# Four of twelve opening filler products on TensorE split into forty 64x64 products

## The chip, the cores and the metric

The kernel runs on one core of one Trainium2 chip. The metric is the device time of one execution in microseconds, from the first to the last thing the core does for it. Three runs of the kernel before gave 791.76, 792.56 and 793.32 us; the median is 792.56 us. Engines are named as in the profile: PE is TensorE's matmul row, PEld its weight load, DVE is VectorE, ACT is ScalarE, POOL is GpSimd, SP is SyncE. An engine's name with a q behind it (SPq, POOLq) is its instruction queue issuing DMAs.

## The reference

Chunked softmax attention on `q`, `k`, `v` of shape 8 x 8 x 576 x 64 (batch, head, position, channel) is followed by a feed-forward layer over the 4608 x 512 result:

```python
q_c, k_c, v_c = (x.reshape(B, H, nc, 64, D) for x in (q, k, v))   # nc = 9 chunks of 64
scores = scale * np.matmul(q_c, k_c.transpose(0, 1, 2, 4, 3))
attn = softmax(scores)                       # over the 64 keys of the same chunk
x = np.matmul(attn, v_c)                     # then laid out as 4608 tokens x 512
h = x @ w_in                                 # 512 -> 2048
g = np.where(h >= 1, h, np.where(h <= -1, 0, (h + 1) ** 2 / 4))
return g @ w_out                             # 2048 -> 512
```

All arrays are float32. The kernel gets near float32 precision out of a faster matmul type by splitting each operand into a high and a low part and adding three products.

## The kernel before, in words

The tokens are worked on in nine tiles of 512. For the first tile (`t = 0`), four pairs of heads are loaded, turned by TensorE against an identity matrix (`flip`, L547, four 128x128 transposes into a PSUM bank), copied to SBUF by ScalarE (L560), multiplied into 64x64 score blocks (`attn_products`, L579), put through a softmax on VectorE, ScalarE and GpSimd (L658 to L674), turned back (L547, copied at L684), multiplied with `v` (L600) and split into a high and a low part (L737, L738). Meanwhile the weights arrive as raw words (`load_weight`, L418, L425) and are split by ScalarE and VectorE (`prepare`, L442 to L471). The feed-forward products of the first three tiles are L788 (in) and L823 (out); later tiles run in pairs through a scheme with fewer products (L1060).

The order on every engine is fixed when the program is built. `Plan.add` collects pieces of work with an engine, an assumed cost and what they need; `Plan.run` places them in time by a list schedule, and calls each piece's `emit` in that order. Each engine then executes its own stream strictly in that order, waiting on semaphores.

Where the plan thinks that TensorE would stand idle early in the program, it puts in a filler: `fill()` in `Plan.run` picks one from a list of (emit, begin, end), and the plan books 0.215 us for it at full pace. A filler is one product of the 128x128 identity (`ident`) with itself into a PSUM bank that real work will overwrite later (`warm`, L1473). Two kinds exist: into `ps_h0` from the start until the first real product of that bank, and into `ps_o0` after that. No result uses a filler's output, and it reads only `ident`, which GpSimd writes first (masks.py:197 and 199). In the profile each float32 product is two passes, and each pass is one weight load (PEld) and one matmul (PE); a transpose is one pass.

The first thing on TensorE is twelve fillers in a row. Behind them stand the transposes of the first pair's `k` and `q`, then fillers and real work in turn.

Of the kernel before, what the change touches and what calls it, by code (L numbers as in the profile page):

```python
# [261 lines left out]
def kernel(  # L262
# [15 lines left out]
    nc = tc.nc  # L278
# [5 lines left out]
    C = 64  # L284
# [12 lines left out]

    EARLY = 2

    BATCH = (0, 1, 2, 3, 4, 5, None, 6, 7)  # L300


# [15 lines left out]
    def buffers(pool, name, n, dtype=F32):  # L318
        return [
            (f"{name}{i}", pool.tile([P, T], dtype, name=f"{name}{i}")) for i in range(n)  # L320
        ]

    ident = sb.tile([P, P], F32, name="ident")
# [43 lines left out]
    h_banks = buffers(psum, "ps_h", 2)  # L367
# [31 lines left out]
    plan = Plan()  # L399
# [79 lines left out]
    def heads_rows(src, t, h):  # L479


        if BATCH[t] is not None:
            return src[BATCH[t], h, :T, :].rearrange("(c p) d -> c p d", p=C)
        return src[:, h, T:, :]
# [10 lines left out]
    def load_blocks(dst, src, t, g, queue):  # L495
# [3 lines left out]
        for j in range(2):  # L499
            for i in range(2):  # L500
                r = (2 * j + i) * Q
                rows = heads_rows(src, t, 2 * g + j)[:, :, i * Q:(i + 1) * Q]
                if BATCH[t] is not None:
                    queue.dma_start(
# [10 lines left out]
    def load_values(dst, src, t, g, queue):  # L515

        for h in range(2):
            rows = heads_rows(src, t, 2 * g + h)
            into = dst[:, h * HALF:(h + 1) * HALF].rearrange("p (n d) -> p n d", d=D)
            if BATCH[t] is not None:  # L520
                queue.dma_start(out=into, in_=rows.rearrange("(n r) p d -> (r p) n d", r=2))
# [5 lines left out]
    def load_heads(t, g, which="qkv"):  # L527
        for n, src, bufs in (("q", q, q_bufs), ("k", k, k_bufs), ("v", v, v_bufs)):
# [4 lines left out]
            parts = 4 if load == load_blocks else 2  # L533
            if BATCH[t] is None:
                parts *= 2
# [297 lines left out]
    def store(t, s):  # L833
# [15 lines left out]
        def send():  # L849
            row = BATCH[t] * S + s * P  # L850
            nc.sync.dma_start(out=out[row:row + P, :], in_=o())
# [620 lines left out]
    def warm(bank):  # L1472
        return lambda: nc.tensor.matmul(  # L1473
            out=bank[:, :P], lhsT=ident, rhs=ident, start=True, stop=True
        )


    plan.emit(("pe", 0.215, 512, (
        (warm(h_banks[0][1]), None, plan.written["ps_h0"][0]),
        (warm(o_banks[0][1]), turned[0], plan.written["ps_o0"][NP]),  # L1480
    )))

# [30 lines left out]
```

## Time and profile before

| what | value |
|---|---|
| median of three runs | 792.56 us (791.76 to 793.32) |
| the profiled execution | 793.6 us, its span from first to last instruction 791.8 us |
| TensorE matmuls (PE) | busy 782.8 us, 99% of the span, 5626 instructions |
| TensorE weight loads (PEld) | busy 646.2 us, 82%, 5626 instructions |
| VectorE | 659.9 us, 83% |
| ScalarE | 523.4 us, 66% |
| GpSimd | 178.4 us, 23% |
| mean granted TensorE clock | 0.999 |

The times in the trace are counted from the span's start. The profiled execution took 1.8 us more than its span, and 1.0 us more than the median run. A matmul's end is modelled, so the starts of the weight loads are the safer clock for TensorE's pace. Where the trace merges instructions into one row, the row gives the first start and the time until the last end. "issue" as a releaser means that the profile shows nothing that the engine waited for.

### The profile page before, as it was taken

The numbers are of one execution on the slowest core, as the hardware profiler recorded it, in microseconds if no ns is written. First come the engines' busy times: TensorE is split into PE (matmuls) and PEld (weight loads), VectorE is DVE, ScalarE is ACT, GpSimd is POOL, SyncE is SP. The second block draws the span as 40 slices with busy tenths as digits, with TensorE's granted clock in tenths as the row PEclk, the third lists the DMA queues.
The fourth block names the chain that finished last, engine by engine and source line by source line (L and its number), as shares of the span: only waits on it lengthen the run. The fifth ranks groups of instructions, "written<-read, shape, count | busy, mean of one in ns | idle before, by whom it ended". The sixth has DMA issues, their size and how long they took to land.

```text
span 791.8 us, 15101 instructions
## 1 busy us (share of the span) xinstructions
PE 782.8 (99%) x5626; PEld 646.2 (82%) x5626; DVE 659.9 (83%) x1013; ACT 523.4 (66%) x903; POOL 178.4 (23%) x294
## 2 busy tenths in 40 slices
PE   9999999999999999999999999999999999999997
PEld 8788888878878888887887888888888888888886
DVE  4889998898679889998769999887699976755796
ACT  5998975444445456886579667865797658657851
POOL 1000005743234433222111112121112111211211
PEclk9999999999999999999999999999999999999999
DMA  9896869858799867898899879989766896666664
GB/s 207 221 359 152 252 136 289 290 174 234 190 277 278 219 170 232 246 299 229 225 243 240 225 210 271 273 226 241 204 198 185 220 260 207 191 192 191 183 207 106
DMA packets 254664, 177.16 MB, mean 224 GB/s; under 512 B 211968, under 2 KB 220160, under 8 KB 254592
## 3 DMA queue, kind: packets, MB, share of 16 engines
q0 software_dynamic: 33344, 117.98, 47.4%
q1 hardware_dynamic: 216992, 57.18, 32.0%
q10 hardware_dynamic: 4256, 1.05, 0.7%
q8 instruction: 44, 0.72, 0.4%
q14 instruction: 28, 0.23, 0.1%
HBM read 133.17 MB, written 38.80 MB: 217 GB/s over the span
## 4 chain that ended last, share of the span: by engine, by line
PE 83%; DVE 7%; ACT 4%; DMA 3%; SPq 1%; issue 1%; ACTq 0%; DVEq 0%
PE ps_o L1060 39%; PE ps_o L823 14%; PE ps_h L788 14%; PE ps_h L1060 12%; PE ps_a L579 2%; DMA aT_both<-qT_both 2%; PE ps_h L600 1%; DVE big_wo L1111 1%; DMA k_sb_both<-in_k_dram 1%; ACT big_wo L1110 1%; ACT big_wo L1107 1%; DMA words_wi<-in_moe_w_in_dram 1%; SPq L490 1%; SPq L722 0%; PE ps_o L600 0%
## 5 line engine op out<-in xcount | busy, mean ns | idle before, releaser
L968 POOL DMA_DIRECT2D big_wi<-mixed x144 | 76.8, 534 | 325.7 <-PE ps_o L1060 178.2
L788 PE MATMUL ps_h<-xh,parts_wi 128*128 128x512 f32 x376 | 123.9, 392 | 0.1
L823 PE MATMUL ps_o<-parts_wo,gh 128*128 128x512 f32 x384 | 119.5, 392 | 0.0
L1060 PE MATMUL ps_o<-big_wo,big_wi 128*128 128x512 f32 x396 | 95.6, 389 | 0.0
L1060 PE MATMUL ps_o<-gh,big_wi 128*128 128x512 f32 x264 | 88.6, 391 | 0.4 <-ACT big_wo L1075 0.3
L1060 PEld LDWEIGHTS ps_o<-big_wo,big_wi 128*128 128x128 f32 x396 | 74.3, 188 | 15.5
L788 PEld LDWEIGHTS ps_h<-xh,parts_wi 128*128 128x128 f32 x376 | 70.6, 188 | 16.5 <-DVE r L799 1.2
L823 PEld LDWEIGHTS ps_o<-parts_wo,gh 128*128 128x128 f32 x384 | 71.4, 188 | 15.3 <-issue 0.3
L1060 PE MATMUL ps_h<-big_wi,big_wi 128*128 128x512 f32 x312 | 75.9, 390 | 0.0
L823 PE MATMUL ps_o<-parts_wo,gl 128*128 128x512 f32 x192 | 74.8, 390 | 0.0
L788 PE MATMUL ps_h<-xl,parts_wi 128*128 128x512 f32 x188 | 73.3, 390 | 0.1
L1060 PE MATMUL ps_o<-big_wi,big_wi 128*128 128x512 f32 x282 | 70.8, 391 | 0.7 <-ACT tmp L1075 0.4
L1060 PEld LDWEIGHTS ps_h<-big_wi,big_wi 128*128 128x128 f32 x312 | 58.4, 188 | 12.2
L1167 ACT CAST big_wo<-big_wo 128x512 fp32r<-128x512 f32 x76 | 47.2, 622 | 31.6 <-PE ps_o L1060 19.9
L1060 PEld LDWEIGHTS ps_o<-big_wi,big_wi 128*128 128x128 f32 x282 | 52.6, 188 | 12.8 <-ACT tmp L1075 1.3
L1167 ACT CAST gh<-big_wo 128x512 fp32r<-128x512 f32 x76 | 47.2, 621 | 23.2 <-PE ps_o L1060 18.2
L1168 DVE TENSOR_TENSOR big_wo<-big_wo,big_wo 128x512 fp32r<-128x512 f32 x76 | 51.6, 684 | 11.6 <-ACT big_wo L1167 11.6
L1110 ACT ACTIVATE big_wo<-big_wo 128x512 f32<-128x512 f32 x96 | 59.8, 632 | 1.9
L1060 PEld LDWEIGHTS ps_o<-gh,big_wi 128*128 128x128 f32 x264 | 49.5, 188 | 12.0 <-ACT big_xl L753 0.8
L1168 DVE TENSOR_TENSOR gl<-big_wo,gh 128x512 fp32r<-128x512 f32 x76 | 51.6, 683 | 8.6 <-ACT gh L1167 8.5
L795 ACT ACTIVATE r<-ps_h 128x512 f32<-128x512 f32 x47 | 28.1, 597 | 36.4 <-PE ps_h L788 36.2
L1060 PE MATMUL ps_o<-gl,big_wi 128*128 128x512 f32 x132 | 51.4, 390 | 0.0
(269 smaller groups left out, 1648.9 us busy)
## 6 DMA issues: line engine op xcount, KB each, us to landing
big_wi<-mixed POOLq DMA_DIRECT2D x144, 512.0 KB, 4.7
big_wo<-mixed POOLq DMA_DIRECT2D x24, 512.0 KB, 4.3
words_wi<-in_moe_w_in_dram SPq DMA_DIRECT2D x16, 512.0 KB, 7.0
words_wo<-in_moe_w_out_dram SPq DMA_DIRECT2D x16, 512.0 KB, 8.8
v_sb<-in_v_dram SPq DMA_DIRECT2D x60, 128.0 KB, 4.0
q_sb_both<-in_q_dram SPq DMA_DIRECT2D x112, 64.0 KB, 3.9
k_sb_both<-in_k_dram SPq DMA_DIRECT2D x112, 64.0 KB, 3.1
mixed<-parts_wi POOLq DMA_DIRECT2D x24, 256.0 KB, 4.2
```

The lines of the kernel that those rows point to most:

```text
L490: queue.dma_start(out=dst[j * C:(j + 1) * C], in_=heads_rows(src, t, 2 * g + j).rearrange("c p d -> p c d"),)
L579: nc.tensor.matmul(out=scores[i * C:(i + 1) * C, half, n * C:(n + 1) * C], lhsT=qT[rows, at], rhs=kT[rows, at], start=True, stop=True,)
L600: nc.tensor.matmul(out=values[half][h * C:(h + 1) * C, n * C:(n + 1) * C], lhsT=v_sb[rows, of:of + C], rhs=rhs, start=True, stop=True,)
L788: nc.tensor.matmul(out=ps, lhsT=weight["wi", j][:, half, kc * P:(kc + 1) * P], rhs=x(), start=(kc == 0 and i == 0), stop=(kc == KC - 1 and ...
L795: plan.add("act", 0.48, lambda: nc.scalar.activation(out=r, in_=ps, func=AF.Relu, bias=0.5, scale=0.5), (pkey,), (rkey,))
L823: nc.tensor.matmul(out=acc, lhsT=x[:, cols], rhs=weight["wo", j][:, half, :], start=(j == 0 and i == 0), stop=(j == NF - 1 and i == 2),)
L968: nc.gpsimd.dma_start(out=place_of(tag).bitcast(F32), in_=mixed[n][:, rows, :])
L1060: nc.tensor.matmul(out=bank, lhsT=parts[part], rhs=rhs, start=fresh and begin and k == 0, stop=end and k == 2, skip_group_check=not fresh,)
L1107: plan.add("act", 0.5, lambda: nc.scalar.activation(out=r(), in_=h(), func=AF.Relu, bias=0.5, scale=0.5), (hkey,), (rkey,))
L1110: plan.add("act", 0.52, lambda: nc.scalar.square(out=r(), in_=r()), (), (rkey,))
L1167: plan.add("act", 0.52, lambda: nc.scalar.copy(out=h(), in_=x()), (key,), (hkey,))
L1168: plan.add("dve", 0.6, lambda: nc.vector.tensor_tensor(out=l(), in0=x(), in1=h().bitcast(F32), op=ALU.subtract), (key, hkey), (lkey,))
```

## The change

The first four calls of the filler into `ps_h0` no longer emit one 128x128 product. Each emits ten products of 64x64 blocks of the identity instead, alternating between the upper half (rows 0 to 63, result in partitions 0 to 63) and the lower half (rows 64 to 127, result in partitions 64 to 127). From the fifth call on the filler is what it was. The plan still books the same cost for each call, so that the order of everything else is the same.

```diff
+    OPENING, SMALL = 4, 5
...
+    fills = itertools.count()
+
+    def opening():
+        bank = h_banks[0][1]
+        if next(fills) >= OPENING:
+            return warm(bank)()
+        for half in [0, 1] * SMALL:
+            rows = slice(half * C, (half + 1) * C)
+            nc.tensor.matmul(out=bank[rows, :C], lhsT=ident[rows, :C], rhs=ident[rows, rows], start=True, stop=True)
+
     plan.emit(("pe", 0.215, 512, (
-        (warm(h_banks[0][1]), None, plan.written["ps_h0"][0]),
+        (opening, None, plan.written["ps_h0"][0]),
         (warm(o_banks[0][1]), turned[0], plan.written["ps_o0"][NP]),
     )))
```

This is the start of TensorE's stream before, from the program's first instruction to the first scores (products are counted here, not passes; `ps_h` is the bank that fillers write, `ps_o` takes the transposes, `ps_a` the scores):

```order
L1508 UNCONDITIONAL_BRANCH
L1473 MATMUL ps_h_93<-ident 128x128 x12
L547 MATMUL ps_o_92<-ident,k_sb_both 128x128 x4
L547 MATMUL ps_o_91<-ident,q_sb_both 128x128 x4
L1473 MATMUL ps_h_93<-ident 128x128 x4
L579 MATMUL ps_a<-kT_both,qT_both 64x64 x16
```

And this is the same place of TensorE's stream in the changed program, whose line numbers are 1 to 14 higher:

```order
L1519 UNCONDITIONAL_BRANCH
L1487 MATMUL ps_h_93<-ident 64x64 x40
L1474 MATMUL ps_h_93<-ident 128x128 x8
L548 MATMUL ps_o_92<-ident,k_sb_both 128x128 x4
L548 MATMUL ps_o_91<-ident,q_sb_both 128x128 x4
L1474 MATMUL ps_h_93<-ident 128x128 x4
L580 MATMUL ps_a<-kT_both,qT_both 64x64 x16
```

Forty small products have come in ahead, and eight of the twelve large ones are left behind them. That is 80 passes for 8, or 144 instructions more, counting weight loads and matmuls. The rest of TensorE's stream and the streams of the other four engines are the same, row for row.

## Rows read from the trace of the kernel before

**Rows 1.** The page: span, busy time, share and instructions of each engine.
```profile
span 791.8 us, 15101 instructions
PE 782.8 (99%) x5626; PEld 646.2 (82%) x5626; DVE 659.9 (83%) x1013; ACT 523.4 (66%) x903; POOL 178.4 (23%) x294
```
**Rows 2.** The chain that ended last, 0 to 30 us: start us, us, what.
```profile
1.50 4.51 DMA k_sb_both<-in_k_dram
...
10.48 4.79 DMA words_wi<-in_moe_w_in_dram
...
15.29 0.68 ACT tmp L442
...
17.06 0.54 DVE tmp L450
...
25.02 0.69 DVE xl L738
25.71 0.04 issue
25.75 1.43 PE ps_h L788 x5
```
**Rows 3.** Waits of TensorE's weight loads over the whole run: us, times, longest.
```profile
PEld ps_o L600 <- DMA k_sb_both<-in_k_dram: 0.4, 1, 0.4
```
**Rows 4.** Weight loads in order of time, 1.3 to 4.9 us: start, us, what.
```profile
1.37 3.70 PEld L1473 LDWEIGHTS ps_h<-ident 128*128 128x128 f32 x17 [1.37 <-POOL ident masks.py:199]
```
**Rows 5.** The same view, 4.95 to 6.9 us (its first load began earlier).
```profile
4.74 1.12 PEld L1473 LDWEIGHTS ps_h<-ident 128*128 128x128 f32 x8
```
**Rows 6.** All engines in order of time, 5.9 to 9 us.
```profile
6.12 0.42 PEld L547 LDWEIGHTS ps_o<-ident,k_sb_both 128*128 128x128 f32 x4 [0.27 <-issue]
...
6.95 0.97 PEld L1473 LDWEIGHTS ps_h<-ident 128*128 128x128 f32 x8
...
8.04 0.56 PEld L579 LDWEIGHTS ps_a<-kT_both,qT_both 64*64 64x64 f32 x32
...
8.66 0.42 PEld L547 LDWEIGHTS ps_o<-ident,k_sb_both 128*128 128x128 f32 x4
...
8.80 0.69 DVE L658 TENSOR_REDUCE mx_both<-ps_a 128x8 f32<-128x512 f32 x1 [8.80 <-PE ps_a L579]
```
**Rows 7.** Weight loads in order of time, 7.9 to 8.6 us.
```profile
7.73 0.19 PEld L1473 LDWEIGHTS ps_h<-ident 128*128 128x128 f32 x1
```
**Rows 8.** Stretches: us, busy (count) of each engine, PEclk, DMA share, GB/s.
```profile
2.00:4.00 2.00, 2.00 (x11) 2.00 (x11) 0.00 (x0) 0.45 (x1) 0.00 (x0) 1.00 0.90 185
7.00:8.00 1.00, 1.00 (x10) 0.92 (x8) 0.00 (x0) 0.89 (x2) 0.00 (x0) 1.00 1.37 184
18.00:20.00 2.00, 2.00 (x46) 1.93 (x38) 1.93 (x5) 1.58 (x4) 1.04 (x1) 1.00 1.09 287
20.00:25.00 5.00, 4.73 (x87) 3.81 (x86) 4.93 (x9) 4.86 (x9) 1.04 (x1) 1.00 0.98 297
```
**Rows 9.** Groups by line and shape, 0 to 12 us: busy us, mean ns | idle us.
```profile
L579 PEld LDWEIGHTS ps_a<-kT_both,qT_both 64*64 64x64 f32 x32 | 0.6, 134 | 0.1
```
**Rows 10.** ScalarE in order of time, 6 to 26 us.
```profile
14.45 0.59 ACT L684 COPY aT_both<-ps_o 128x512 f32<-128x512 f32 x1
15.29 0.68 ACT L442 ACTIVATE tmp<-words_wi 128x512 f32<-128x512 f32 x1 [0.26 <-DMA words_wi<-in_moe_w_in_dram]
15.87 0.58 ACT L560 COPY first_wi<-ps_o 128x512 f32<-128x512 f32 x1
16.34 0.69 ACT L445 ACTIVATE words_wi<-words_wi 128x512 uint32<-128x512 uint32 x1
```
**Rows 11.** VectorE in order of time, 6 to 26 us.
```profile
17.06 0.69 DVE L450 SCALAR_TENSOR_TENSOR tmp<-tmp,words_wi 128x512 uint32<-128x512 uint32 x1 [0.89 <-ACT words_wi L445]
```
**Rows 12.** The page's DMA queues: packets, MB, share of 16 engines' span.
```profile
q8 instruction: 44, 0.72, 0.4%
```
**Rows 13.** Weight loads in order of time, 492 to 500 us.
```profile
497.73 0.45 PEld L579 LDWEIGHTS ps_a<-kT_both,qT_both 64*64 64x64 f32 x22
498.62 0.65 PEld L579 LDWEIGHTS ps_a<-kT_both,qT_both 64*64 64x64 f32 x34 [0.45 <-issue]
```
**Rows 14.** Weight loads in order of time, 184.8 to 185.9 us.
```profile
185.59 0.19 PEld L823 LDWEIGHTS ps_o<-parts_wo,gh 128*128 128x128 f32 x1 [0.27 <-issue]
```

## The prediction

> **What bounds the kernel now.** I read four views: the page's busy times, the chain that ended last, TensorE's weight loads in order of time through the first 9 us, and the streams of ScalarE and VectorE up to 26 us. TensorE is busy 99% of the span [rows 1], and from 25.75 us the chain is TensorE's own work with few breaks [rows 2]. So a delay of that point is a delay of the end, unless a later wait for a transfer takes it up. The only such wait on TensorE that the list names is 0.4 us long [rows 3]. Ahead of 25.75 us TensorE is not the bound: the chain goes through the landing of `k` at 6.01, a weight transfer landing at 15.27, then ScalarE's and VectorE's preparation of the weights [rows 2]. The question is what a slower or faster opening of TensorE does to that point.
>
> **The opening before.** Twelve fillers are 24 passes. Seventeen loads start from 1.37 on, the seventeenth at 4.74, where the next view begins [rows 4, 5]: (4.74 - 1.37) / 16 = 0.211 us a pass. Later eight passes of the same fillers take 0.97 us with 0.19 for the last load, so (0.97 - 0.19) / 7 = 0.111 us a pass [rows 6, 7]. The first pace is half the second: 1.2 against 2.4 GHz by the pace. The granted clock's column says 1.00 in both stretches [rows 8], so in the first microseconds I go by the pace. In the eight loads from 4.74 to a last start at 4.74 + 1.12 - 0.19 = 5.67, the seven steps sum to 0.93 us; 1.6 steps of 0.211 and the rest of 0.111 fit that, so the pace doubled at about 5.07, some 3.7 us after the first filler began [rows 5]. The last filler pass is through by 5.78, `k` has landed at 6.01, and the first transpose loads at 6.12 [rows 2, 6]. TensorE had some 0.3 us to spare here.
>
> **The change part by part.**
>
> *Removed:* 8 passes of 128x128 at the slow pace, 8 x 0.211 = 1.69 us.
>
> *Added:* 80 passes of 64x64. The trace has passes of that shape: 32 in the scores, whose loads take 0.56 us with 0.134 for one, so (0.56 - 0.13) / 31 = 0.0139 us a pass at the fast pace [rows 6, 9]. But the scores use four combinations of row half and output half, the new products only two (the upper with the upper, the lower with the lower). If what a pass holds is its quarter of the array, two quarters give half the rate: 0.0277 fast, 0.0555 slow. The ends: if the issue of instructions sets the 0.0139, two quarters cost no more than four (0.0278 slow); if the two halves do not overlap at all, a pass costs half of a large one, 0.0555 fast and 0.1055 slow. I take 0.0555 slow, 0.0277 fast.
>
> The Trainium skill, TensorEngine Tiling (Array Packing), "Key Properties", says that different tiles of the array execute loads and products in parallel, and the section on configurations counts four 64x64 tiles. By this rule a tile is the resource and two tiles run at half the rate of four, which is the value taken; the pace of the scores agrees with four in parallel, no row shows two.
>
> So from 1.37 to 5.07 there are 3.70 / 0.0555 = 67 passes, and the other 13 take 13 x 0.0277 = 0.36 us: 5.43. The change of shape costs a little: the last of the 32 score loads starts at 8.47, the next, larger one at 8.66 [rows 6], 0.15 more than the shape's own step, so 5.58. Sixteen passes of the eight remaining large fillers at 0.111 are 1.78 us: 7.36. The `k` transposes then load at 7.36 in place of 6.12: **+1.24 us**. The spare 0.3 us is used up in this. At the low end (0.0278 slow) the small ones end at 1.37 + 2.22 = 3.59, and 16 passes, the first 6 slow, end at about 6.1: no delay. At the high end 35 passes run by 5.07, 45 more take 2.50 us, then 0.15 and 1.78: 9.50, a delay of 3.4 us.
>
> *What a delay of 1.24 us does to 25.75 us.* The scores, the softmax and the turning back of the first heads follow TensorE, so ScalarE's copy at 14.45 moves to 15.69 and ends at 16.28. Then comes `prepare` at 15.29, which now waits for nothing but the copy. It had idled 0.26 us for the weight transfer [rows 10]: it is late by about 1.24 - 0.26 = 0.98. VectorE at 17.06 waits for the ScalarE step at 16.34, which is behind it in ScalarE's stream [rows 10, 11], so it is late by the same. From 18 to 25 us VectorE is busy 6.86 of 7.00 us, which leaves 0.14 us to catch up with [rows 8], and the chain runs on VectorE until 25.71 [rows 2]. I take **+0.97 us** at 25.75 and at the end. Should the slack at 15.29 not count (another copy, at 15.87, follows TensorE too), it is +1.24; with the 0.4 us of [rows 3] taken up as well, +0.57. The DMA issues on SP and ScalarE at the start load fresh buffers and wait for none of this.
>
> *Moved:* the program's blocks. 44 packets of 0.72 MB are 16 KB each [rows 12], and TensorE's 11,252 instructions [rows 1] by 44 are 256 each: 64 bytes an instruction. The 144 new ones shift every later block edge by 0.56 of a block against the work. Two pauses of TensorE have no releaser in the profile: 0.45 us in the middle of a burst of small products at 498.6 [rows 13], and 0.27 us at 185.6 [rows 14]. If both are late blocks, the shift can remove 0.72 us. It can also put an edge into another burst: two more of the first kind would be +0.90. One lost and one gained, 0, is what I take; the ends are -0.72 and +0.90.
>
> The Trainium skill, Runtime: NRT & Kernel Launch, "Instruction fetch mechanics", says that the stream is refilled in 16 KiB blocks of 256 instructions ahead of need and that an edge is mostly hidden. By the rule this term is 0 at both ends; the packets agree with it in size, the unexplained 0.45 us speaks against "hidden" where a burst eats a block in 128 passes at 0.0139, 1.8 us.
>
> *Sum:* +0.97 + 0 on the profiled execution: 793.6 + 0.97 = 794.6. That execution stands 1.0 us above the median, so for the median 792.56 + 0.97 = **793.5 us**, 0.12% up. A difference of 0.2%, 1.6 us, is about what a measurement of this kernel can tell from none.
>
> **The rivals.**
>
> *The clock does not rise on small products (slower).* The pace doubled 3.7 us after the first 128x128 filler. If products in two quarters of the array do not count as enough work, that time starts behind them: 80 x 0.0555 = 4.44, so they end at 5.81, with the change of shape 5.96, and the rise comes at about 9.7. The 16 large passes then run slow, 16 x 0.211 = 3.38, to 9.34, and three or four more at 0.1 us extra: a delay of about 3.5 us at the transposes, less the slack of 0.26, +3.2: 795.8. For it speaks that only half the array is in use; against it that TensorE is never idle. It decides as soon as the loads of the large fillers, behind the small ones, still come 0.21 us apart beyond 5.1 us.
>
> *The halves don't overlap (slower).* The high end above: +3.4 - 0.26 = +3.1, 795.7. The scores speak against it, since their passes plainly overlap.
>
> *Issue sets the pace (no change).* No delay at the transposes, and the blocks' term alone: 792.6, between 791.8 and 793.5.
>
> *Faster.* The pauses without a releaser go and no others come, with no delay ahead: 792.56 - 0.72 = 791.8, 0.1%. For more than 0.2% the clock would have to rise earlier in the runs than it does in the profiled one, which begins with the rise already 3.7 us after the first pass; nothing in the rows shows such a gain.
>
> **How the numbers follow.** Forecast (+0.6 to +1.3) 0.45; issue sets the pace 0.18; clock late 0.23; no overlap 0.07; faster 0.07. The forecast's own range with the blocks' term is 792.4 to 794.7. With three tenths on the two cases at 795.7 the range has to reach them: 791.8 to 795.9. Slower by over 0.2% (above 794.15): 0.9 of the 0.30 on those two, 0.2 of the forecast's 0.45 (a block pause on top), so 0.27 + 0.09 = 0.36. Faster by over 0.2% (below 790.97): 0.07. Same: 0.57.
>
> **What would show it.** The loads of the small products: 0.055 us apart at first and 0.028 later confirms the two quarters, 0.028 first and 0.014 later the issue's pace. Large fillers 0.111 us apart behind them show the clock. The `k` transposes should load near 7.4, VectorE's step after the first scores should begin near 10.0 in place of 8.80, and the unbroken TensorE chain near 26.7. The pause at 498.6 should be gone, and one or two of like size may stand in other bursts. I am wrong if the transposes start at 6.1 or beyond 9, or if the delay is there at 9 us and gone by 26 us.

## The result, and the profile after

| | before | changed |
|---|---|---|
| median, us | 792.56 (15 runs, 791.39 to 794.53) | 796.25 (15 runs, 793.46 to 802.65) |
| ratio | | 1.0052, 95% interval 1.0036 to 1.0067 |
| profiled execution, its span | 793.6, 791.8 | 796.7, 794.9 |

The change costs 0.52%, 3.7 us. I had forecast 793.5, and the range ended at 795.9: too low. The runs also spread over 9 us where those of before spread over 3.

The page after, against [rows 1, 12]: 72 loads and 72 matmuls more, and one more instruction packet, 45 for 44.

```profile
span 794.9 us, 15245 instructions
...
PE 784.1 (99%) x5698; PEld 648.0 (82%) x5698; DVE 659.9 (83%) x1013; ACT 522.9 (66%) x903; POOL 177.8 (22%) x294
...
q8 instruction: 45, 0.74, 0.4%
```

The opening, as weight loads in order of time (start, us, what), against [rows 4 to 6]:

```profile
1.36 4.34 PEld L1487 LDWEIGHTS ps_h<-ident 64*64 64x64 f32 x80 [1.36 <-POOL ident masks.py:199]
5.82 1.91 PEld L1474 LDWEIGHTS ps_h<-ident 128*128 128x128 f32 x16
7.65 0.47 PEld L548 LDWEIGHTS ps_o<-ident,k_sb_both 128*128 128x128 f32 x4
```

The 80 small loads are (4.34 - 0.13) / 79 = 0.0533 us apart, all at the low pace. The sixteen large ones are 0.11 apart but for the first step or two, so the pace doubled at about 6.0. The `k` transposes load at 7.65 in place of 6.12: 1.53 late.

The chain that ended last, at its joint with TensorE's unbroken work, against [rows 2]:

```profile
26.53 0.69 DVE xl L739
27.22 0.04 issue
27.26 1.42 PE ps_h L789 x5
```

It stands at 27.26 in place of 25.75: 1.51 late. The delay came through nearly whole. Then ScalarE in order of time, against [rows 10]:

```profile
16.02 0.59 ACT L685 COPY aT_both<-ps_o 128x512 f32<-128x512 f32 x1
16.50 0.68 ACT L443 ACTIVATE tmp<-words_wi 128x512 f32<-128x512 f32 x1
```

The wait for the weight transfer is gone, as forecast; `prepare` starts 1.21 late, behind a copy that is 1.57 late. VectorE is 1.50 late again at the step of [rows 11]:

```profile
18.56 0.69 DVE L451 SCALAR_TENSOR_TENSOR tmp<-tmp,words_wi 128x512 uint32<-128x512 uint32 x1 [0.81 <-ACT words_wi L446]
```

Two new stops of TensorE stand further on. One has no releaser, in a burst of 64x64 products:

```profile
386.89 0.83 PEld L580 LDWEIGHTS ps_a<-kT_both,qT_both 64*64 64x64 f32 x49
...
389.01 0.20 PEld L580 LDWEIGHTS ps_a<-kT_both,qT_both 64*64 64x64 f32 x7 [1.29 <-issue]
```

It is the kind of [rows 13], three times as long; that of [rows 13] itself is gone. An instruction packet is under way just ahead of it. This is the DMA view from 386.60 to 387.62 us; from 387.65 on to the end of the pause the view has no such row:

```profile
q8 instruction: 1, 0.02, 6.1%
```

In the trace that packet lands at 387.61, and TensorE goes on 1.40 us later. The other stop waits for VectorE, first in the changed kernel, then in the kernel before:

```profile
157.71 0.19 PEld L824 LDWEIGHTS ps_o<-parts_wo,gl 128*128 128x128 f32 x1
159.72 0.20 PEld L601 LDWEIGHTS ps_h<-aT_both,v_sb 64*64 64x64 f32 x3 [1.83 <-DVE r L800]
```

```profile
156.31 0.19 PEld L823 LDWEIGHTS ps_o<-parts_wo,gl 128*128 128x128 f32 x1
157.09 0.20 PEld L600 LDWEIGHTS ps_h<-aT_both,v_sb 64*64 64x64 f32 x3 [0.60 <-DVE r L799]
```

VectorE has been late since its turning of `q` at 138 us, which waited for a `k` load. VectorE after, and before:

```profile
138.38 1.25 DVE L566 STREAM_TRANSPOSE qT_both<-q_sb_both 128x1024 f32<-128x1024 f32 x1 [4.58 <-DMA k_sb_both<-in_k_dram]
```

```profile
135.74 1.25 DVE L565 STREAM_TRANSPOSE qT_both<-q_sb_both 128x1024 f32<-128x1024 f32 x1 [3.35 <-DMA k_sb_both<-in_k_dram]
```

SyncE's queue takes 7.66 us to issue the eight `k` loads in place of 6.00, again after and before:

```profile
132.04 7.66 SPq L505 DMA_DIRECT2D k_sb_both<-in_k_dram  x8
```

```profile
130.89 6.00 SPq L504 DMA_DIRECT2D k_sb_both<-in_k_dram  x8
```

In the changed kernel's trace an instruction packet lies among them (135.41 to 136.29). Before, the packets around that time were at 120.05 and 148.29.

### The profile page after: what moved, and what is told of

It is laid out like the page before. It is cut to its first block, busy times and chain, and to the rows that moved or that the text cites. A ratio compares the mean times of both kernels' runs of the same rounds, so it can differ in the third digit from the quotient of the medians.

```text
span 794.9 us, 15245 instructions
## 1 busy us (share of the span) xinstructions
PE 784.1 (99%) x5698; PEld 648.0 (82%) x5698; DVE 659.9 (83%) x1013; ACT 522.9 (66%) x903; POOL 177.8 (22%) x294
## 4 chain that ended last, share of the span: by engine, by line
PE 84%; DVE 8%; ACT 4%; DMA 2%; issue 1%; SPq 1%; POOL 0%; ACTq 0%; POOLq 0%; DVEq 0%
PE ps_o L1061 39%; PE ps_o L824 14%; PE ps_h L789 13%; PE ps_h L1061 12%; PE ps_a L580 2%; PE ps_h L601 1%; DMA k_sb_both<-in_k_dram 1%; DVE big_wo L1112 1%; ACT big_wo L1111 1%; ACT big_wo L1108 1%; PE ps_h L1474 1%; DMA aT_both<-qT_both 1%; DVE r L800 1%; PE ps_h L1487 1%; PE ps_o L548 1%
```

## Where the time went, in one table

To add this up I compared each real TensorE load (all but the fillers) with the same load of the kernel before, trace against trace. "Late" is how much later it starts, the median over 4 us around that time:

| trace | late at 8 us | 33 | 150 | 165 | 380 | 420 | 510 | 780 |
|---|---|---|---|---|---|---|---|---|
| changed | 1.58 | 1.54 | 1.40 | 2.62 | 2.57 | 3.52 | 2.81 | 3.10 |

So in this execution the opening brought 1.5, the wait at 157 us (where TensorE stops, 157.9 to 159.7) 1.2 and the pause at 389 us 1.4, of which 0.45 came back by 420; between 495 and 505 us, around the pause of [rows 13] that is now gone, 0.6 came back. Smaller steps of up to 0.3 us cancel. Sum: 3.1 us, the difference of the two profiled executions. Is the pattern of the stops chance, or does it belong to the 144 instructions? The experiments put this to the test. One theory, called **opening**, says that the late transposes are the loss; the other, **edges**, says that it is the shift of the program's 256-instruction blocks against the work. An edge is the point where one block ends and the next begins.

## The experiments

Each edit is shown against the changed kernel, and each kernel ran beside the kernel before, whose medians were 792.2 (first four), 792.39 (next four) and 792.37 (last three). No output depends on any of the edited products. "Shift" is the number of instructions (loads and matmuls) that the edit puts ahead of the real work beyond those of the kernel before.

**The changed kernel once more**, unaltered.

> The changed program, unaltered, for a second trace and more times. Two theories stand. Edges: what is lost beyond the 1.5 us of the later opening is pauses in bursts of small products, at the places where the shifted blocks of TensorE's instructions end. It expects 795.5 to 797 us, a pause without a releaser again in the burst near 387 us at the same count of instructions, of another length (0.5 to 3 us). Opening: the later opening alone costs it all, through the waits that it leads to. It expects the same time, and the pause of 387 us gone or at another count.

Measured: 795.49 us, ratio 1.0037 (1.0025 to 1.0050). The wait at 157 us is there again, 2.09; the pause at 389 is not. So where TensorE pauses differs between executions of one program, and a single trace shows one draw of it.

**All four quarters of the array.** Same count, shift 144.

```diff
-        for half in [0, 1] * SMALL:
...
+        for n in range(2 * SMALL):
+            rows = slice(n % 2 * C, (n % 2 + 1) * C)
+            outs = slice(n // 2 % 2 * C, (n // 2 % 2 + 1) * C)
...
+                out=h_banks[n % 2][1][outs, :C], lhsT=ident[rows, :C], rhs=ident[rows, rows], start=True, stop=True
```

> The same forty small products at the same place, but going round all four quarters of the array (two PSUM banks) in place of two: 144 instructions more as in the change, at twice the pace, so that the transposes of k wait for their data as before (6.1 to 6.4 us). Edges expects some 2 us over the kernel before, 794 to 795.5, with the pause near 386 us. Opening expects the time of the kernel before, 792 to 793.2. If a quarter of the array is not what a small product holds, the loads are 0.055 us apart as in the change and the opening is as late as there.

Measured: 796.03 us, 1.0052 (1.0033 to 1.0070). Weight loads in order of time:

```profile
1.36 2.63 PEld L1488 LDWEIGHTS ps_h<-ident 64*64 64x64 f32 x80 [1.36 <-POOL ident masks.py:199]
4.11 3.33 PEld L1474 LDWEIGHTS ps_h<-ident 128*128 128x128 f32 x16
7.36 0.47 PEld L548 LDWEIGHTS ps_o<-ident,k_sb_both 128*128 128x128 f32 x4
```

(2.63 - 0.13) / 79 = 0.0316 us a pass against 0.0533 over two quarters: the quarters work side by side. But the large fillers run at 0.21 to the end, the pace doubles only at 7.2, and the transposes are late all the same. As a test of the shift alone it is spoilt. The wait at 157 (2.24) and a pause at 388.73 (1.00) are back.

**Late without a shift.** Each of the first four fillers is one product of 448 columns.

```diff
-        for half in [0, 1] * SMALL:
-            rows = slice(half * C, (half + 1) * C)
...
+            out=bank[:, :7 * C].rearrange("p (n c) -> p n c", c=C), lhsT=ident,
+            rhs=ident[:, :C].rearrange("p (n c) -> p n c", n=1).broadcast_to([P, 7, C]), start=True, stop=True,
```

> The first four fillers are one product each with 448 columns in place of 128: no instruction more, but an opening that ends 0.9 to 1.9 us later. Edges expects the opening's cost alone, 793.5 to 794.5, the pauses of the kernel before (498.6 plus the delay) and none near 387. Opening expects the whole loss of the change, 795.5 to 797.

Measured: 795.38 us, 1.0033 (1.0020 to 1.0045); transposes at 8.17, 2.05 late. The wait at 157 is as before (0.62), nothing stands at 389. The time is above the 794.5 at most that edges expected and just under the 795.5 at least of opening; the opening was also later than the 0.9 to 1.9 us that I had put in. A late opening does cost time at the end, without any shift.

**Late, and a whole block.** All twelve fillers become 76 small products: 256 instructions more, so that every later edge stands where it stood.

```diff
-        if next(fills) >= OPENING:
+        n = next(fills)
+        if n >= 12:
...
+        for half in ([0, 1] * SMALL)[:8 if n < 2 else 6]:
```

> All twelve fillers are small products, 76 in all: 256 instructions more, exactly one block, so that the edges stand against the later work as in the kernel before, and an opening about as late as in the change (transposes of k near 7.8 us). Edges expects 793.5 to 794.5 us, no pause near 387 and the pause near 500 back. Opening expects 795.5 to 797.

Measured: 794.22 us, 1.0023 (1.0014 to 1.0032), transposes at 7.46. The wait at 157 is gone (0.35), and the pause of [rows 13] is back at its old place in the work:

```profile
496.97 0.45 PEld L580 LDWEIGHTS ps_a<-kT_both,qT_both 64*64 64x64 f32 x22
...
498.88 0.44 PEld L580 LDWEIGHTS ps_a<-kT_both,qT_both 64*64 64x64 f32 x23 [1.47 <-issue]
```

As many as 256 instructions more cost less than 144.

**Shift 144 with the transposes on time.** The first fifteen fillers become 51 small products: thirteen of them four each (the last one three), and two are dropped. The first forty products are thus those of the change, but they stand for ten fillers instead of four, with no large one behind them.

```diff
-        if next(fills) >= OPENING:
+        n = next(fills)
+        many = 4 if n < 10 or n in (12, 13) else 0 if n < 12 else 3 if n == 14 else None
+        if many is None:
...
-        for half in [0, 1] * SMALL:
+        for half in ([0, 1] * SMALL)[:many]:
```

> The first ten fillers are four small products each (one large filler's time), two are left out, and three of the next group are small: 144 instructions more, as in the change, with an opening that ends as before (transposes of k at 6.1 to 6.4 us). Theory of the edges, as the traces so far give it: the shift costs by itself, in two ways, a block of instructions that arrives near 135 us while k is loaded (VectorE 1.2 to 1.6 us late there, and TensorE near 157) and a late block in the burst near 386 us (0 to 1.5 us); the pause at 498 us goes. It expects 793.2 to 794.7 us. Theory of the opening: nothing is late at the start, so 791.7 to 792.8.

Measured: 796.27 us, 1.0047 (1.0029 to 1.0066), transposes at 5.60, TensorE 0.12 late at 33 us. This is the loss of the change without its late opening: the opening theory, as the main cause, falls. Edges had the loss too small as well (794.7 at most). The wait at 157 and a pause, longer than any other, are in its trace, in two views:

```profile
158.23 0.20 PEld L601 LDWEIGHTS ps_h<-aT_both,v_sb 64*64 64x64 f32 x3 [1.76 <-DVE r L800]
```

```profile
327.37 0.61 PEld L580 LDWEIGHTS ps_a<-kT_both,qT_both 64*64 64x64 f32 x33
...
330.28 0.31 PEld L580 LDWEIGHTS ps_a<-kT_both,qT_both 64*64 64x64 f32 x11 [2.30 <-issue]
```

**Shifts 256, 112 and 64, transposes on time.** The same edit, with `many` as here in turn:

```diff
+        many = 0 if n in (10, 11) else 4 if n < 24 else None
...
+        many = 0 if n in (10, 11) else 4 if n < 10 else None
...
+        many = 4 if n < 6 else 0 if n < 8 else None
```

> Twenty-two small-product fillers in the time of the large ones, two left out: 256 instructions more, one whole block, opening on time. Both theories expect the kernel before: 791.7 to 792.8 us, no wait over 0.5 us near 157, no pause near 386, the pause near 498 at its old count plus 256. If small products cost something besides (the clock, say), this is slower by itself.

> The first ten fillers are four small products each, two are left out, the rest as before: 112 instructions more, opening on time. Edges: 32 instructions less of a shift than the change put the block that came near 135 us at about 137 to 139, behind k's landing, and the edge of the burst near 386 out of its end; the pause at 498 goes too: 791.3 to 792.4 us. A theory by which more instructions in front cost in proportion expects 0.8 of the shift of 144.

> Six fillers are four small products each, two are left out, four stay: 64 instructions more, opening on time. Edges: no block near 135 us (about 142), none late at 386 or 498; other bursts can meet an edge near their end (183, 213, 431 or 548 us): 791.3 to 793.5 us.

Measured: 793.64 us, 1.0016 (1.0007 to 1.0026); 793.88, 1.0019 (1.0008 to 1.0029); 795.63, 1.0035 (1.0018 to 1.0052). All three came out slower than I expected. The smallest shift costs most, so the loss doesn't go with the number of instructions. Shift 64's trace has two pauses, at 85.71 (0.73) and here:

```profile
304.45 0.19 PEld L824 LDWEIGHTS ps_o<-parts_wo,gh 128*128 128x128 f32 x1
...
306.96 0.19 PEld L824 LDWEIGHTS ps_o<-parts_wo,gh 128*128 128x128 f32 x1 [2.33 <-issue]
```

It is no longer inside the burst but one load behind it.

**Fewer instructions, and the same edges by more.** Twelve fillers as six products of 256 columns (24 instructions fewer); sixteen as four of 512 columns (48 fewer); and small products again for 232 more, which puts the edges where 24 fewer puts them.

```diff
+        wide = 1 if n >= 12 else 2 if n % 2 == 0 else 0
...
+        wide = 1 if n >= 16 else 4 if n % 4 == 0 else 0
...
+        many = 0 if n in (10, 11) else 4 if n < 22 else None
```

In the first two, `wide` is the number of 128-column copies of the identity in one product.

> The first twelve fillers become six products of 256 columns: 24 instructions less, the same time on TensorE (a pass of 448 columns took 3.5 times one of 128), so an opening on time. Every pause of TensorE without a releaser so far stands at a count of instructions that leaves 192 by 256, where this falls into the last 70 instructions of a burst of small products or shortly behind one. Shifted by 24 less, 13 of 16 bursts have the edge elsewhere; the bursts near 159, 407 and 498 us keep it at place 209 to 232 of 256. Edges expects 791.0 to 792.8 us, no slower than before, with at most one such pause. A theory by which small products cost by themselves expects the kernel before, too: this run tells whether the phase can also give something back.

> The first sixteen fillers become four products of 512 columns: 48 instructions less, the same time on TensorE. 13 of 16 bursts are free of an edge near their end; those near 159, 407 and 498 us have it at 233 to 256 of 256. Edges expects 791.0 to 793.5 us, a pause of 0 to 1.5 us near 498 or 407.

> Twenty fillers of four small products each in their time, two left out: 232 instructions more, which against the blocks is the same phase as 24 less. Edges expects the time of the run with 24 less, within 0.15%, and its pauses at the same bursts. If small products or more instructions cost by themselves, this is slower than that run by more.

Measured: 792.38 us, 0.9993 (0.9984 to 1.0002); 793.45, 1.0009 (1.0001 to 1.0018); 793.42, 1.0009 (0.9998 to 1.0021). With 24 fewer, the trace has no pause as long as that of [rows 13], and the kernel is level with the one before; 232 more, which has the same edges, is 0.13% above it by the medians, as edges expected; but its trace has a pause of 0.98 us at 497.83, where the trace of 24 fewer has none. With 48 fewer two pauses stand in the trace, at 161.12 (1.37) and 499.45 (0.85). No version beats the kernel before by what can be told.

**All together.** "Late at 33 us" is from each trace as in the table above; "lost" is the median less that of before; the last column is their difference, what the opening does not account for.

| shift | opening edit | late at 33 us | lost | lost less late |
|---|---|---|---|---|
| -24 | 256 columns | 0.11 | 0.0 | -0.1 |
| -48 | 512 columns | 0.31 | 1.1 | 0.8 |
| 0 | 448 columns | 2.40 | 3.2 | 0.8 |
| 232 | small, on time | 0.36 | 1.1 | 0.7 |
| 256 | small, on time | 0.83 | 1.25 | 0.4 |
| 256 | small, late | 1.25 | 2.0 | 0.8 |
| 112 | small, on time | 0.81 | 1.5 | 0.7 |
| 64 | small, on time | 0.56 | 3.2 | 2.7 |
| 144 | small, on time | 0.12 | 3.9 | 3.8 |
| 144 | four quarters | 1.22 | 3.8 | 2.6 |
| 144 | the change | 1.54 | 3.7 | 2.2 |
| 144 | the change again | 1.71 | 3.3 | 1.6 |

Two groups stand apart. At seven of the settings the loss is the delay of the opening and under 1 us more. At shifts 144 and 64 it is 1.6 to 3.8 more. (A median's interval is 1.0 to 1.5 us to either side at shift 144, and each delay is from one execution, so the last column is good to a microsecond or so.) The delay and the edges do not simply add: with shift 144, on time and late cost the same within the intervals.

The edges can also be seen. I count every record of TensorE from the program's start: loads, matmuls, and the semaphore and drain instructions among them (193 in the kernel before). All 14 pauses without a releaser of 0.45 us or more behind 25 us, in the trace of before and the twelve others, stand at a count that leaves 193 or 194 when divided by 256. Loads and matmuls alone do not line up: they leave anything from 88 to 178.

| trace | records ahead of the pause | packet lands, us | TensorE goes on, us |
|---|---|---|---|
| before | 8130 = 31 x 256 + 194 | 497.33 | 498.62 |
| changed | 6593 = 25 x 256 + 193 | 387.61 | 389.01 |
| 256, late | 8386 = 32 x 256 + 194 | 497.36 | 498.88 |
| 144, on time | 5825 = 22 x 256 + 193 | 328.89 | 330.28 |
| 64, on time | 5313 = 20 x 256 + 193 | 305.51 | 306.96 |

In each of these rows TensorE goes on 1.3 to 1.5 us after a packet has landed. All edges together settle what the pauses are. Take every place with such a count as an edge, and give the edges their packets in order, the first packet to the second edge (before has 44 edges and 44 packets). Behind 25 us the 13 traces have 542 edges. At 19 of them TensorE pauses without a releaser, for 0.11 to 2.33 us, and each time it goes on 1.0 to 1.6 us after the edge's packet has landed. At the other 523 the packet had landed 1.9 us or more before, and no such pause stands there (only, at one of them, the 0.35 us that TensorE idles ahead of most bursts). So the pauses are late blocks. All 19 are among the 129 edges that lie in a burst of small products or just behind one (60 or more of the 70 loads ahead are small); 14 of the 129 pause for 0.45 us or more. An edge that the shift puts into a burst is a draw, at about one in nine.

The wait at 157 us goes with the shift too: 1.76 to 2.24 us in the four traces with shift 144, 0.62 at most in the nine others. In those four the packet starts 3.4 to 3.9 us behind the first of the eight `k` loads, and their issue takes 7.66 to 7.87 us; in the others it takes 5.49 to 6.78. At shift 112 the packet starts 4.3 behind, and no long wait follows. The landings fit this more closely. Four transfers of turned data (L722) stand in SyncE's queue just ahead of the `k` loads. With shift 144 on time the third of them lands at 133.24, 5.38 us after its issue (5.61 before); the packet is under way from 133.90 to 134.78; the fourth lands 8.12 us after its issue in place of 6.34, and the first `k` load 0.40 later. For the fourth it is 8.44 and 8.60 us in two more traces with shift 144 (the changed kernel's shows no landing), and 5.98 to 6.95 in the nine others. At shift 112 the packet starts only 0.55 us ahead of that landing. Still, nothing was run that moves the packet without the rest: that it slows these transfers is argued, not shown.

## Why the prediction was wrong

**What failed is the term *Moved*:** "One lost and one gained, 0, is what I take; the ends are -0.72 and +0.90." I had the blocks, their size, the shift of 0.56 of a block and the right reading of [rows 13] and [rows 14] (the 0.27 us too stands at an edge). That a block is 256 came out of 11,252 loads and matmuls by 44; the records to be counted are 11,445, 260 by 44, but the edges do stand 256 of them apart. And I priced another edge in a burst at the one such pause that the trace showed, 0.45 us. It is one draw: what an edge costs is how late its packet lands, and one trace doesn't tell that. The same kind took 1.29, 1.47, 2.30 and 2.33 us in other traces, and at the very place of [rows 13] it took 1.47 in one program and none in another with its edges in the same place (448 columns). And a block has a second way to cost: 1.2 to 1.6 us more in the wait at 157 us, which goes with the shift. With the opening on time the loss beyond the delay is +3.8 us in the median, four times the term's upper end. Up to 0.8 us of this kind stands at other shifts too, so some 3 us of it belong to the shift of 144.

The rule that I weighed it against, the Trainium skill, Runtime: NRT & Kernel Launch, "Instruction fetch mechanics", has the edge mostly hidden. Most edges agree: no trace shows more than two pauses of 0.45 us or more at its 44 or so edges. At some edges in or just behind a burst the measurement decides against it, with up to 2.33 us.

**The opening was right in kind and too small.** The two quarters were right: 0.0533 us a pass against the 0.0555 taken, and four quarters give 0.0316. That agrees with the rule of the Trainium skill, TensorEngine Tiling (Array Packing), "Key Properties", though four quarters were 1.7 times as fast as two, not twice. What I had wrong is the moment of the doubled pace, 5.07 taken over from before and 6.0 found. It isn't the small products that hold it back as such: the last 24 of the same 80 small loads, here in the changed kernel and then with the products spread, took

```profile
4.30 1.40 PEld L1487 LDWEIGHTS ps_h<-ident 64*64 64x64 f32 x24
```

```profile
4.31 1.04 PEld L1489 LDWEIGHTS ps_h<-ident 64*64 64x64 f32 x24
```

so the pace doubled near 4.9 in the second, behind the same instructions. +1.24 became +1.53 at the transposes.

**The slack of 0.26 at ScalarE** was there, but I stopped at it: the second copy, which I named as the bound of 1.24, decided. In ScalarE's stream of the changed kernel it waits for TensorE, and starts 1.49 behind its 15.87 of before:

```profile
17.36 0.58 ACT L561 COPY first_wi<-ps_o 128x512 f32<-128x512 f32 x1 [0.17 <-PE ps_o L548]
17.84 0.69 ACT L446 ACTIVATE words_wi<-words_wi 128x512 uint32<-128x512 uint32 x1
```

The step behind it, for which VectorE waits, is 1.50 late, and so is VectorE: not 0.97 (0.98 by its own subtraction).

**"A delay of that point is a delay of the end"** holds in the medians as far as the table tells. In single traces it need not: with 256 instructions more, late, TensorE was 1.25 late at 33 us and 0.04 at 300.

**The rivals.** Issue as what sets the pace falls (the passes were 0.0533 apart, not 0.0278). No overlap falls (they were not 0.1055 apart). Faster falls, since the kernel is slower. The late clock is not what the changed kernel's trace shows: its large fillers are 0.11 apart by 6.1 us, not by 9.7. With four quarters it came partly true, 0.21 apart until 7.2.

**What I would change in the working:** the chance of slower was 0.36 because I put the cost of the shift within 1 us. The spread of one observed pause is not a bound; with some 44 edges, any of which the shift could put into a burst, the bound above had to be two or three pauses, each as long as a packet that starts late and lands (two of 1.4 us and the delay of 1.24 would have given 796.6).

## What to carry to other kernels

Instructions added in front can cost more than their own time where the stream behind them has bursts of short instructions: they move every later block edge, and which edges fall into a burst, and which of these pause, is then a new draw. Before such a change is judged, time the same shift without it; here the shift of 144 alone cost what the whole change cost. A count near a multiple of 256 keeps the edges where they were: 232, 256 and 24 fewer cost under 1 us beyond the delay that came with them. So did 112 and 48 fewer, so a small cost does not need a whole block.

## What was not expected of the hardware

- A pause of TensorE at a block edge can be 2.33 us, though the packet itself takes about 1 us (304.51 to 305.51): it was started late. At the 542 edges a packet starts from 4.7 us ahead to 8.3 us behind the moment at which TensorE reaches the edge before. Why it starts when it does stays open.
- The pace of TensorE doubled between 3.5 and 5.9 us after its first pass in these programs (4.9 us in one, 7.2 in another), though in both its loads had followed one another without a wait until then. In two traces of the changed kernel it was 6.0 and 6.4 us into the span.
- Six of the 40 runs with shift 144 had a mean granted clock of 0.995 to 0.997 and took 797.3 to 802.65 us; no run of another program listed here was under 0.998, nor one of the kernel before whose clock is on record. None of the six was traced, so where the clock fell, and whether a pause set it off, stays open. Without them the changed kernel's first 15 runs have a median of 795.6 us in place of 796.25, so most of the loss is elsewhere.
- One pass of 448 columns took 0.75 us at the low pace, 2 cycles a column at 1.2 GHz (448 x 2 / 1200 = 0.747). The loads of such products, in order of time:

```profile
3.77 0.34 PEld L1485 LDWEIGHTS ps_h<-ident 128*128 128x128 f32 x1 [0.41 <-issue]
4.51 0.34 PEld L1485 LDWEIGHTS ps_h<-ident 128*128 128x128 f32 x1 [0.41 <-issue]
5.26 0.30 PEld L1485 LDWEIGHTS ps_h<-ident 128*128 128x128 f32 x1 [0.41 <-issue]
```
